# Block sums of the second weights, made where the second and third chunk's tokens lay

## The chip, the cores and the metric

The kernel runs on one core of a Trainium2 chip. Its engines are TensorE (PE in the profile, PEld for its weight loads), VectorE (DVE), ScalarE (ACT), GpSimd (POOL) and SyncE (SP), which here issues all DMA. Each engine takes its instructions strictly in the order in which the program has them. The metric is device time in microseconds (us), lower is better, as a median over runs.

## The reference

The kernel computes a windowed attention and feeds its result to a two-layer feed-forward network:

```python
scores = scale * np.matmul(q, k.transpose(0, 1, 3, 2))      # 8 batches, 8 heads, 576 positions, 64 wide
mask_plain = (rel >= 0) & (rel < window)                    # heads 0 to 3, window 32
mask_dil = (rel >= 0) & (rel < window * dilation) & (rel % dilation == 0)   # heads 4 to 7, dilation 4
scores = np.where(masks[None, :, :, :], scores, -1000000000.0)
attn = softmax(scores); attn_out = np.matmul(attn, v)
...
h = x @ w_in                       # x: 4608 tokens x 512, w_in: 512 x 2048
g = h * np.clip(h + 3.0, 0.0, 6.0) / 6.0
return g @ w_out                   # w_out: 2048 x 512
```

## The kernel before, in words

The 4608 tokens are cut into 12 chunks of 384. Every fp32 operand of the feed-forward part is split into a high and a low part of type fp32r, and a product is three matmuls: high by high, high by low, low by high.

**The first four chunks** are multiplied plainly, in 64 steps of a chunk and one 128-wide slice f of the hidden layer. `gemm1` (L545 to L547) makes `ps_h` in one of two PSUM banks, ScalarE makes `t` by `relu` (L553), VectorE the gate (L556, which reads `ps_h` and so frees its bank), GpSimd the high part `gh`, VectorE the low part `gl` (L564), and two steps later `gemm2` (L595 to L597) uses them. So the gate of a step must be done before the gemm1 two steps later can start.

**The other eight chunks** are multiplied by a Strassen-like scheme of seven products, in groups of two chunks. It needs, besides the weights themselves, sums of blocks of both weight matrices. These are made from the weights on the chip while the first four chunks run, once for each of eight pairs k of slices of both weights (side 0 is `w_in`, side 1 `w_out`): `combo_words` adds high and low part into a tile `v` (L640, two VectorE instructions), `combo_sum` makes four sums in place (L648, four instructions), `combo_high` casts them into a second tile `sh` (L652, ScalarE), `combo_low` leaves the low part in `v` (L657, VectorE), and `combo_out` stores `sh` and `v` into DRAM (L675, two DMAs of 512 KB, into `sums` for side 0 and `rights` for side 1). `combo_plain` stores the plain weights beside them (L666, three DMAs for each pair). Later a ring of eight slots loads all this back (L689, `ring<-sums` and `ring<-rights`), 512 KB at a time.

**Places.** The tokens of the first four chunks lie in three blocks x0, x1, x2 of four tiles each (high and low of two kinds), chunk 3 again in x0. They are allocated once for the whole program (`tokens_tile`, from the pool `const`). When chunk 1 is done, x1's tiles are used for the raw tokens of chunks 4 and 5 (`raw_of`); when chunk 2 is done, x2 takes the operands S2 and S1 of the seven products (`cell`). The block sums take two slots, `v` and `sh`, of the pool `w` (36 slots), which also holds the weights and the ring.

**The order.** A hand-written list orders the first 29 steps. After it every piece of work is an entry of a plan with an engine, a cost, what it comes after, and what slots it takes and gives (`op`, `transfer`). `_in_time` puts the entries of each engine in order by simulating the plan, and the program then issues each engine's instructions in just that order. A plan's costs are guesses of the author's: for instance, a pair's `combo_plain` counts as 1.35 us of SP, and a store as landed 2.6 us after its transfer. On the chip the waits are semaphores: an instruction that writes a place waits until every reader of the place's last content is done, and the instructions behind it on its engine wait with it. DMAs signal eight semaphores in turn, `DMAHW0` to `DMAHW7`.

Of the kernel before, what the change touches and what calls it, by code (L numbers as in the profile page):

```python
# [86 lines left out]
def windowed_attention_ffn(ctx: ExitStack, tc: tile.TileContext, qk, vp, w, mask, out, out_t):  # L87
# [55 lines left out]


    def tokens_tile(block, kind, part, name, dtype=F32R):
        return const.tile([P, 2, CH], dtype, name=name, tag=f"x{block}{kind}{int(part)}")

    xh, xl = ([[tokens_tile(block, kind, part, f"x{block}") for kind in range(2)] for block in range(3)] for part in (1, 0))
    mi = const.tile([P, mask.shape[1]], BF16, name="mi")
# [34 lines left out]
    def w_tile(name, shape, dtype=F32):  # L184
        return wpool.tile([P, *shape], dtype, name=name, tag="w")
# [218 lines left out]
    def raw_of(block, kind):  # L404

        if (block, kind) not in raws:
            if block < 2:
                raws[block, kind] = tokens_tile(1, kind, (xl, xh)[block] is xh, "raw", F32)
            else:
                raws[block, kind] = w_tile("raw", [2, CH])  # L410
        return raws[block, kind]
# [220 lines left out]
    ]  # L632
    KEPT = (T1, T3, T4, T2, R11, R21, R22)

    def combo_words(side, k, i, eng):

        if (side, k) not in combos:
            combos[side, k] = w_tile("v", [4, HALF])
        x, v = (win, wout)[side][2 * k + i], combos[side, k]
        eng.tensor_tensor(  # L640
            out=v[:, 2 * i : 2 * i + 2].rearrange("p a n -> p (a n)"), in0=x[:, 0].bitcast(F32), in1=x[:, 1].bitcast(F32), op=ALU.add
        )
# [5 lines left out]
        eng.tensor_tensor(out=v[:, to], in0=v[:, a], in1=v[:, b], op=op)  # L648

    def combo_high(side, k):  # L650
        hi = w_tile("sh", [4, HALF], F32R)
        nc.scalar.copy(hi, combos[side, k])  # L652
        combos[side, k] = combos[side, k], hi

# [38 lines left out]
    def cell(g, i):  # L693

        if i in (A11, A12, S3):
            x = (i, min(g, 1)) if i == A11 else (i, 0)
            if x not in cells:
                second_place = lambda part, kind: tokens_tile(1, kind, part, "cell")
                small = lambda: w_tile("cell", [2, CH], F32R)
                cells[x] = {  # L700
                    (A11, 0): lambda: [second_place(1, 0), small()], (A12, 0): lambda: [second_place(0, 0), second_place(1, 1)],
                    (A11, 1): lambda: [cells[A11, 0][0], second_place(0, 1)], (S3, 0): lambda: [small(), small()],
                }[x]()
            return cells[x]
        block, kind = {S2: (2, 0), S1: (2, 1), A22: (0, 0), S4: (0, 1)}[i]
        return [x[block][kind] for x in (xh, xl)]

    sources = {}
# [112 lines left out]
    def attend(bs, pools):  # L821
# [38 lines left out]
        for tv in values:  # L860
# [11 lines left out]
            if tv + NLOAD < T:  # L872
                landed_v[tv + NLOAD] = transfer(0.4, 0.77, lambda tv=tv: load_v(tv + NLOAD), [beat])
            pieces = [(n, token // CH) for _, n, _, _, token in spans(tv)]
            x = [*x, ends_of[1]] if any(PLAIN <= c < PLAIN + 2 for n, c in pieces) else x
            touched = {c for n, c in pieces if c >= PLAIN + 2} - {c for c, kind in raw_seen if kind == trios[tv][1]}
            raw_seen.update((c, trios[tv][1]) for c in touched)
            plain = [n for n, c in pieces if c < PLAIN]
# [28 lines left out]
    words, combined, taken = {}, {}, {}  # L907

    def combine(side, k):
        x = op("DVE", 0.69, lambda: combo_words(side, k, 0, nc.vector), takes=[("w", 2, SPARE[side][k])], ahead=LEAD_SUMS)  # L910
        words[side, k] = x = op("DVE", 0.69, lambda: combo_words(side, k, 1, nc.vector), [x], ahead=EVER)
        for i in range(4):
            x = op("DVE", 0.42, lambda i=i: combo_sum(side, k, i, nc.vector), [x], ahead=EVER)
        x = op("ACT", 1.05, lambda: combo_high(side, k), [x], ahead=EVER)
        x = op("DVE", 1.25, lambda: combo_low(side, k, 0, 1, nc.vector), [x], ahead=EVER)
        combined[side, k] = [
            transfer(0.9, 2.0, lambda: combo_out(side, k), [x], gives=[("w", 2)]),
            transfer(1.35, 1.5, lambda: combo_plain(side, k), ahead=EARLY),
        ]

# [58 lines left out]
    def fill(g, free_after):  # L979
# [5 lines left out]
        source = {A11: b11, A12: b21, S2: [t2], S1: [t1], S3: [t3], A22: [t4], S4: b22}  # L985
        after = {A11: [t1], A12: [t4], S2: [t4], S1: [t2], S3: [], A22: [], S4: [t2, t3]}
        order = (S3, A11, S2, S1, A22, S4, A12) if g == 0 else range(PRODUCTS)
        for i in order:
            before_high = [filled.get((0, S3)), *([filled[0, A11], filled[0, S4]] if i == A12 else ()), t1, t2, t3, t4] if g == 0 and i in (A11, A12) else ()
            x = op("ACT", 0.85, lambda i=i: fill_high(g, i), [*source[i], free_after[i], *before_high], takes=[("w", {S3: 2, A11: 1}[i])] if g == 0 and i in (S3, A11) else ())  # L990
            filled[g, i] = op("DVE", 1.1, lambda i=i: fill_low(g, i), [x, *after[i]], gives=() if g == 0 and i in (A11, A12, S3, S4) else SLOT)

    def old_unit(n, tt):
# [288 lines left out]
    with tc.manual_schedule(  # L1282
# [12 lines left out]
            n += kind == "G"  # L1295
        assert len(converted) == 2 * NF

        free = {"work": WORK, "w": SLOTS_W - 2 * NF, "ps_h": 2, "ps_a": 0}
        free["work"] -= 2 * sum(m not in done for m in range(n))
        ends_of, firsts, b = {}, {}, 0  # L1300
        for side in range(2):
# [2 lines left out]
        for m in range(n, len(steps)):  # L1304
# [3 lines left out]
            for late in range(2):  # L1308
                if (m, late) in SPOTS:
                    attend((b, b + 1), (ps_h, ps_a, ps_a, ps_a))  # L1310
                    b += 2
                if not late and m - LAG not in done:
                    second(m - LAG)
        for at in range(RING):
            bring(at)
        spare = {0: ends_of[PLAIN - 1], 1: ends_of[1], 2: ends_of[2]}
# [231 lines left out]
```

## Time and profile before

| what | value |
|---|---|
| runs | 833.76, 834.25, 837.03 us; median 834.25 us |
| the profiled execution | 835.44 us, of it 833.7 us of span |
| TensorE busy | 818.5 us, 98% of the span |
| VectorE, ScalarE, GpSimd busy | 646.6, 579.3, 124.2 us |
| mean granted TensorE clock | 0.996 |
| DMA moved | 214.71 MB, 73.7% of 16 engines' span on the main queue |
| first four chunks | to about 326 us |
| seven products of the first group, first layer | about 326.6 to 398 us |

A row of the page's groups names line, engine, operation, output<-inputs, shapes, count, then busy us and mean ns of one, then the idle time ahead of them and what ended it. A row of a timeline has the start, the us until the last of its instructions ended, engine, line, operation and count; an instruction can start before the end of the one ahead, since engines pipeline. SPq is SyncE's DMA-issuing queue: its durations are the time to issue, not to transfer.

### The profile page before, as it was taken

How to read it: one execution, taken by the hardware profiler on the slowest of the kernel's cores; microseconds unless marked ns; L12 is line 12 of the kernel's file. 1: busy time of each engine (PE TensorE's matmuls, PEld its weight loads, DVE VectorE, ACT ScalarE, POOL GpSimd, SP SyncE). 2: the span in 40 equal slices, each digit the busy share in tenths (PEclk: the TensorE clock that was granted, in tenths of full speed). 3: DMA queues.
4: the chain of work that ended last, by engine and by line, in shares of the span. 5: the costliest groups of instructions: out<-in, count | busy, mean ns of one | idle time of the engine just before them, and what ended most of it. 6: DMA issues, size and time to landing. Idle time of an engine off the chain costs nothing.

```text
span 833.7 us, 22177 instructions
## 1 busy us (share of the span) xinstructions
PE 818.5 (98%) x8732; PEld 772.6 (93%) x8732; DVE 646.6 (78%) x1266; ACT 579.3 (69%) x1406; POOL 124.2 (15%) x184
## 2 busy tenths in 40 slices
PE   7899999999999999999899999999999999999998
PEld 4788999898999998999899999999999999999998
DVE  4899996656777988888899786898676898345983
ACT  4788775344898884988859799855698855345552
POOL 1238442111222221000103002000011000000000
PEclk9899999999999999999999999999999999999999
DMA  8757433262678999999986798787798777897381
GB/s 295 237 205 235 127 113 122 69 228 93 195 249 284 301 344 356 353 395 395 389 282 232 273 346 302 266 315 274 262 316 303 251 266 257 307 359 238 116 297 58
DMA packets 115784, 214.71 MB, mean 258 GB/s; under 512 B 7520, under 2 KB 40288, under 8 KB 115680
## 3 DMA queue, kind: packets, MB, share of 16 engines
q1 hardware_dynamic: 115680, 213.29, 73.7%
q8 instruction: 69, 1.13, 0.6%
q14 instruction: 35, 0.29, 0.1%
HBM read 174.47 MB, written 38.80 MB: 256 GB/s over the span
## 4 chain that ended last, share of the span: by engine, by line
PE 86%; DMA 8%; DVE 3%; ACT 1%; issue 1%; SPq 0%; POOL 0%; DVEq 0%; POOLq 0%
PE ps_o L745 28%; PE ps_x L754 8%; PE ps_x L755 7%; PE ps_x L756 7%; PE ps_h L545 5%; PE ps_o L596 5%; PE ps_o L597 5%; PE ps_o L595 5%; PE ps_h L546 5%; PE ps_h L547 5%; DMA st<-in_w 1%; PE ps_b L246 1%; DMA ring<-sums 1%; DMA ring<-rights 1%; DMA rights<-sh 1%; PE ps_a L246 1%
## 5 line engine op out<-in xcount | busy, mean ns | idle before, releaser
L745 PE MATMUL ps_o<-gh,ring 128*128 128x384 f32 x896 | 230.4, 334 | 1.6 <-DMA ring<-rights 1.2
L745 PEld LDWEIGHTS ps_o<-gh,ring 128*128 128x128 f32 x896 | 161.9, 188 | 2.2 <-DMA ring<-rights 1.5
L745 PE MATMUL ps_o<-gl,ring 128*128 128x384 f32 x448 | 150.0, 335 | 0.9 <-DVE gl L1208 0.9
L1208 DVE TENSOR_TENSOR gl<-g,gh 128x384 fp32r<-128x384 f32 x224 | 116.6, 557 | 18.4 <-ACT gh L1204 15.9
L1204 ACT CAST gh<-g 128x384 fp32r<-128x384 f32 x224 | 105.4, 513 | 34.6 <-PE ps_o L745 26.6
L754 PE MATMUL ps_x<-x,ring 128*128 128x384 f32 x256 | 88.4, 345 | 0.0
L545 PE MATMUL ps_h<-x,wi 128*128 128x384 f32 x256 | 88.2, 345 | 0.0
L546 PE MATMUL ps_h<-x,wi 128*128 128x384 f32 x256 | 86.3, 337 | 0.0
L547 PE MATMUL ps_h<-x,wi 128*128 128x384 f32 x256 | 86.2, 337 | 0.0
L755 PE MATMUL ps_x<-x,ring 128*128 128x384 f32 x256 | 86.1, 336 | 0.0
L756 PE MATMUL ps_x<-x,ring 128*128 128x384 f32 x256 | 86.1, 336 | 0.0
L745 PEld LDWEIGHTS ps_o<-gl,ring 128*128 128x128 f32 x448 | 84.1, 188 | 1.8 <-DVE gl L1208 1.8
L596 PE MATMUL ps_o<-wo,gh 128*128 128x512 f32 x192 | 74.8, 390 | 0.5 <-DVE wo L529 0.5
L595 PE MATMUL ps_o<-wo,gh 128*128 128x512 f32 x192 | 74.9, 390 | 0.0
L597 PE MATMUL ps_o<-wo,gl 128*128 128x512 f32 x192 | 74.7, 389 | 0.0
L553 ACT ACTIVATE t<-ps_h,three 128x384 f32<-128x384 f32 x64 | 37.1, 583 | 50.6 <-PE ps_h L547 50.1
L494 POOL TENSOR_SCALAR va<-st 128x512 f32<-128x512 f32 x32 | 54.7, 1718 | 76.1 <-DMA st<-in_w 63.5
L756 PE MATMUL ps_x<-cell,ring 128*128 128x384 f32 x192 | 64.9, 338 | 0.0
L755 PE MATMUL ps_x<-cell,ring 128*128 128x384 f32 x192 | 64.7, 337 | 0.0
L754 PE MATMUL ps_x<-cell,ring 128*128 128x384 f32 x192 | 64.7, 337 | 0.0
L1173 DVE TENSOR_TENSOR g<-g 128x768 f32<-128x768 f32 x64 | 60.6, 954 | 0.0
L292 ACT ACTIVATE e<-e,mx 128x64 f32<-128x64 f32 x216 | 59.9, 345 | 0.2
(108 smaller groups left out, 1775.4 us busy)
## 6 DMA issues: line engine op xcount, KB each, us to landing
ring<-sums SPq DMA_DIRECT2D x112, 512.0 KB, 8.5
ring<-rights SPq DMA_DIRECT2D x112, 512.0 KB, 6.7
st<-in_w SPq DMA_DIRECT2D x32, 512.0 KB, 4.4
kq<-in_qk SPq DMA_DIRECT2D x39, 416.0 KB, 4.9
v<-in_v SPq DMA_DIRECT2D x39, 390.0 KB, 6.4
sums<-wi SPq DMA_DIRECT2D x24, 256.0 KB, 6.7
rights<-wo SPq DMA_DIRECT2D x24, 256.0 KB, 4.5
out<-o SPq DMA_DIRECT2D x15, 384.0 KB, 2.8
```

Of the source, the lines that this page charges most:

```text
L545: nc.tensor.matmul(ph, lhsT=wt(f, 0)[:, ks], rhs=a, start=(kt == 0), stop=False)
L546: nc.tensor.matmul(ph, lhsT=wt(f, 0)[:, ks], rhs=b, start=False, stop=False)
L547: ins = nc.tensor.matmul(ph, lhsT=wt(f, 1)[:, ks], rhs=a, start=False, stop=(kt == NK - 1))
L595: nc.tensor.matmul(po[c][tt], lhsT=gh[:, rows], rhs=wt(f, 2), start=first, stop=False)
L596: nc.tensor.matmul(po[c][tt], lhsT=gh[:, rows], rhs=wt(f, 3), start=False, stop=False)
L597: return nc.tensor.matmul(po[c][tt], lhsT=gl[:, rows], rhs=wt(f, 2), start=False, stop=(f == NF - 1))
L745: nc.tensor.matmul(banks[part][:, :CH], lhsT=right[:, a, cols], rhs=x, start=(start and not i), stop=(i == 2), skip_group_check=True)
L754: nc.tensor.matmul(bank, lhsT=tile_[:, 0, ks], rhs=h[:, kt], start=(start and kt == 0), stop=False, skip_group_check=True)
L755: nc.tensor.matmul(bank, lhsT=tile_[:, 0, ks], rhs=l[:, kt], start=False, stop=False, skip_group_check=True)
L756: nc.tensor.matmul(bank, lhsT=tile_[:, 1, ks], rhs=h[:, kt], start=False, stop=(kt == 1), skip_group_check=True)
L1204: nc.scalar.copy(two[0], gated_tile(g, q, k))
L1208: nc.vector.tensor_tensor(out=two[1], in0=gated_tile(g, q, k), in1=two[0].bitcast(F32), op=ALU.subtract)
```

## The change

The three blocks of tokens become pools of their own, which are released and allocated anew (`room`, `stage_of`). Block 1 holds chunk 1's tokens, then the block sums of the second weights' pairs 0 to 3, then the raw tokens of chunks 4 and 5. Block 2 holds chunk 2's tokens, then the block sums of the second weights' pairs 4 to 7, then the operands S2 and S1. As a pool of block sums a block has three slots of 4 KB a partition, of which a pair takes two. Side 1 takes no slot of `w` for its sums any more. The raw tokens of chunks 4 and 5 wait for the stores of pairs 0 to 3, and the first group's operands for those of pairs 4 to 7.

```diff
     def tokens_tile(block, kind, part, name, dtype=F32R):
-        return const.tile([P, 2, CH], dtype, name=name, tag=f"x{block}{kind}{int(part)}")
+        return rooms[block].tile([P, 2, CH], dtype, name=name, tag=f"x{block}{kind}{int(part)}")
+
+    def room(block, name, bufs=1):
+
+        if block in rooms:
+            rooms[block].release()
+        side = "right" if block == 2 else "left"
+        rooms[block] = tc.alloc_tile_pool(name=name, bufs=bufs, side=side, reuse_waits="tile")
...
             if block < 2:
+                stage_of(1, 2)
                 raws[block, kind] = tokens_tile(1, kind, (xl, xh)[block] is xh, "raw", F32)
...
+    stage = {1: 0, 2: 0}
+
+    def stage_of(block, n):
+
+        if stage[block] < n:
+            for x in (xh, xl) if n == 1 else ():
+                x[block] = None
+            room(block, f"{'-cr'[n]}{block}", 3 if n == 1 else 1)
+            stage[block] = n
+
+    def combo_tile(side, k, name, dtype=F32):
+
+        if not side:
+            return w_tile(name, [4, HALF], dtype)
+        block = 1 + k // 4
+        stage_of(block, 1)
+        return rooms[block].tile([P, 4, HALF], dtype, name=name, tag="c")
...
-            combos[side, k] = w_tile("v", [4, HALF])
+            combos[side, k] = combo_tile(side, k, "v")
...
-        hi = w_tile("sh", [4, HALF], F32R)
+        hi = combo_tile(side, k, "sh", F32R)
...
-            x = [*x, ends_of[1]] if any(PLAIN <= c < PLAIN + 2 for n, c in pieces) else x
+            if any(PLAIN <= c < PLAIN + 2 for n, c in pieces):
+                x = [*x, ends_of[1], *(combined[1, k][0] for k in range(4))]
...
     def combine(side, k):
-        x = op("DVE", 0.69, lambda: combo_words(side, k, 0, nc.vector), takes=[("w", 2, SPARE[side][k])], ahead=LEAD_SUMS)
+        slots = f"x{1 + k // 4}" if side else "w"
+        x = op(
+            "DVE", 0.69, lambda: combo_words(side, k, 0, nc.vector), takes=[(slots, 1, 1)] if side else [(slots, 2, SPARE[side][k])],
+            ahead=LEAD_SUMS,
+        )
...
-        x = op("ACT", 1.05, lambda: combo_high(side, k), [x], ahead=EVER)
+        x = op("ACT", 1.05, lambda: combo_high(side, k), [x], takes=[(slots, 1)] if side else (), ahead=EVER)
...
-            transfer(0.9, 2.0, lambda: combo_out(side, k), [x], gives=[("w", 2)]),
+            transfer(0.9, 2.0, lambda: combo_out(side, k), [x], gives=[(slots, 2)]),
...
-            x = op("ACT", 0.85, lambda i=i: fill_high(g, i), [*source[i], free_after[i], *before_high], ...
+            x = op("ACT", 0.85, lambda i=i: fill_high(g, i), [*source[i], free_after[i], *(in_room if g == 0 else ()), *before_high], ...
...
-        free = {"work": WORK, "w": SLOTS_W - 2 * NF, "ps_h": 2, "ps_a": 0}
+        free = {"work": WORK, "w": SLOTS_W - 2 * NF, "ps_h": 2, "ps_a": 0, "x1": 0, "x2": 0}
...
+        for c in (1, 2):
+            plan[ends_of[c]].gives.append((f"x{c}", 3))
```

TensorE's order is the same. The others move; in the rows of the change a line number is by 12 to 41 higher for the same code (L683 is `combo_high`'s cast, L652 before; L706 is `combo_out`, L675 before; L697 is `combo_plain`, L666 before; L566 is `relu`, L553 before; L569 is the gate, L556 before).

On SP, around the 24 stores of the plain second weights. Before:

```order
L196 DMA kq<-in_qk 128x832 x2
L205 DMA v<-in_v 128x780 x2
L666 DMA rights<-wo 256x1x256 x24
L689 DMA ring<-sums 128x2x512
L196 DMA kq<-in_qk 128x832
L205 DMA v<-in_v 128x780
L196 DMA kq<-in_qk 128x832
L205 DMA v<-in_v 128x780
L675 DMA sums<-sh 128x4x256
L675 DMA sums<-v 128x4x256
```

and of the change:

```order
L208 DMA kq<-in_qk 128x832 x2
L217 DMA v<-in_v 128x780 x2
L706 DMA rights<-sh 128x4x256
L706 DMA rights<-v 128x4x256
L697 DMA rights<-wo 256x1x256 x24
L720 DMA ring<-sums 128x2x512
L208 DMA kq<-in_qk 128x832
L217 DMA v<-in_v 128x780
L208 DMA kq<-in_qk 128x832
L706 DMA rights<-sh 128x4x256
L706 DMA rights<-v 128x4x256
```

Pair 5's store now stands ahead of the 24, and pair 6's behind them, where a store of side 0 stood. The eight stores of side 1 stood two ahead of this place and six behind it before; now five stand ahead of the 24, one more is the first pair shown here, one is the second, and the last follows three DMAs later.

On ACT, in the steps that follow those stores' time. Before (`relu` is `t<-ps_h`; `e` and `x` belong to the attention):

```order
L553 ACTIVATE t_4627<-ps_h_4576,three_92 128x384 [waits PE_49]
L292 ACTIVATE e_4597<-e_4597,mx_4609 128x64 [waits Activation_49,Pool_49]
L292 ACTIVATE e_4597<-e_4597,mx_4609 128x64
L311 ACTIVATE x_4637<-ps_a_4457,z_4630 128x64 [waits DVE_49,Activation_49]
L311 ACTIVATE x_4637<-ps_a_4457,z_4630 128x64
L292 ACTIVATE e_4597<-e_4597,mx_4609 128x64 x2
L311 ACTIVATE x_4637<-ps_a_4457,z_4630 128x64 x2
L292 ACTIVATE e_4597<-e_4597,mx_4609 128x64 x2
L725 CAST cell_4667<-raw_4593 128x768 [waits DMAHW1_49,DVE_49]
L553 ACTIVATE t_4683<-ps_h_4640,three_92 128x384 [waits PE_49]
```

and of the change (`sh_4734` is pair 7's; `t_4722` and `t_4770` are the `t` of the 59th and 60th `relu` of 64):

```order
L566 ACTIVATE t_4722<-ps_h_4682,three_101 128x384 [waits PE_49,Pool_49]
L304 ACTIVATE e_4648<-e_4648,mx_4702 128x64 [waits Pool_49]
L304 ACTIVATE e_4648<-e_4648,mx_4702 128x64
L323 ACTIVATE x_4728<-ps_a_4508,z_4719 128x64 [waits DVE_49,Activation_49]
L323 ACTIVATE x_4728<-ps_a_4508,z_4719 128x64
L683 CAST sh_4734<-v_4488 128x1024 [waits DMAHW2_49]
L304 ACTIVATE e_4648<-e_4648,mx_4702 128x64 x2
L323 ACTIVATE x_4728<-ps_a_4508,z_4719 128x64 x2
L304 ACTIVATE e_4648<-e_4648,mx_4702 128x64 x2
L566 ACTIVATE t_4770<-ps_h_4737,three_101 128x384 [waits PE_49,Activation_49]
```

Pair 7's cast now stands between two `relu`s, and it waits for a DMA. The tile it writes lies where `sh_4612`, pair 6's, lay. On SP, with buffer numbers, the store of that tile:

```order
L208 DMA kq_4638<-in_qk 128x832 [waits DMAHW7_49,PE_49]
L217 DMA v_4642<-in_v 128x780 [waits DMAHW0_49]
L208 DMA kq_4646<-in_qk 128x832 [waits DMAHW1_49,PE_49]
L706 DMA rights_117<-sh_4612 128x4x256 [waits DMAHW2_49,Activation_49]
L706 DMA rights_117<-v_4170 128x4x256 [waits DMAHW3_49,DVE_49]
L217 DMA v_4670<-in_v 128x780 [waits DMAHW4_49]
L720 DMA ring_4696<-sums_116 128x2x512 [waits DMAHW5_49,Pool_49]
L720 DMA ring_4732<-sums_116 128x2x512 [waits DMAHW6_49]
L706 DMA rights_117<-sh_4734 128x4x256 [waits DMAHW7_49,Activation_49]
L706 DMA rights_117<-v_4488 128x4x256 [waits DMAHW0_49,DVE_49]
```

A DMA takes the semaphore that it waits for in its own turn, so `rights<-sh_4612` is the one that signals `DMAHW2`, and the cast waits for its landing. Pair 6's store (from `sh_4612`, `v_4170`) is the one behind the 24.

More of the change, by code (lines that the diff above doesn't have):

```diff
@@ L145, in tokens_tile @@
     def tokens_tile(block, kind, part, name, dtype=F32R):
-        return const.tile([P, 2, CH], dtype, name=name, tag=f"x{block}{kind}{int(part)}")
+        return rooms[block].tile([P, 2, CH], dtype, name=name, tag=f"x{block}{kind}{int(part)}")
[4 more added lines that the diff above has]
+        rooms[block] = tc.alloc_tile_pool(name=name, bufs=bufs, side=side, reuse_waits="tile")
+    rooms = {}
+    for block in range(3):
+        room(block, f"x{block}")
+        ctx.callback(lambda block=block: rooms[block].release())
     xh, xl = ([[tokens_tile(block, kind, part, f"x{block}") for kind in range(2)] for block in range(3)] for part in (1, 0))
@@ L705, in cell @@
         block, kind = {S2: (2, 0), S1: (2, 1), A22: (0, 0), S4: (0, 1)}[i]
+        if stage[2] < 2:
+            stage_of(2, 2)
+            for part, x in ((1, xh), (0, xl)):
+                x[2] = [tokens_tile(2, kind, part, "x2") for kind in range(2)]
         return [x[block][kind] for x in (xh, xl)]
@@ L987, in fill @@
         order = (S3, A11, S2, S1, A22, S4, A12) if g == 0 else range(PRODUCTS)
+        in_room = [combined[1, k][0] for k in range(4, 8)]
         for i in order:
             before_high = [filled.get((0, S3)), *([filled[0, A11], filled[0, S4]] if i == A12 else ()), t1, t2, t3, t4] if g == 0 and i in (A11, A12) else ()
-            x = op("ACT", 0.85, lambda i=i: fill_high(g, i), [*source[i], free_after[i], *before_high], takes=[("w", {S3: 2, A11: 1}[i])] if g == 0 and i in (S3, A11) else ())
+            x = op("ACT", 0.85, lambda i=i: fill_high(g, i), [*source[i], free_after[i], *(in_room if g == 0 else ()), *before_high], takes=[("w", {S3: 2, A11: 1}[i])] if g == 0 and i in (S3, A11) else ())
             filled[g, i] = op("DVE", 1.1, lambda i=i: fill_low(g, i), [x, *after[i]], gives=() if g == 0 and i in (A11, A12, S3, S4) else SLOT)
```

## The prediction

> **What bounds the kernel now.** I read the page's head and chain of waits first, then TensorE's waits, then the timelines of SP, ACT, DVE and PE around the places where the order changes.
>
> ```profile
> span 833.7 us, 22177 instructions
> PE 818.5 (98%) x8732; PEld 772.6 (93%) x8732; DVE 646.6 (78%) x1266; ACT 579.3 (69%) x1406; POOL 124.2 (15%) x184
> PE 86%; DMA 8%; DVE 3%; ACT 1%; issue 1%; SPq 0%; POOL 0%; DVEq 0%; POOLq 0%
> ```
>
> TensorE is busy for 98% of the span, and its order stays as it was. So the time can change only where TensorE comes to wait, ceases to wait, or gets another clock. Its waits from 330 us to the end (engine, tile, line, releaser: us in total, times, longest):
>
> ```profile
> PE ps_o L745 <- DMA ring<-rights: 1.2, 1, 1.2
> PE ps_o L745 <- DVE gl L1208: 0.9, 3, 0.5
> PE ps_o L745 <- ACT gh L1204: 0.4, 1, 0.4
> ```
>
> They lie in one place, the switch from the first to the second layer of the first group of products. By stretches of time (window, its us, busy us of PE, PEld, DVE, ACT and POOL with counts, TensorE's granted clock, DMA share, GB/s):
>
> ```profile
> 309.00:321.00 12.00, 12.00 (x63) 11.02 (x62) 10.39 (x17) 6.47 (x19) 2.93 (x3) 1.00 1.05 384
> 397.00:400.00 3.00, 1.79 (x11) 1.46 (x10) 2.65 (x8) 2.35 (x6) 0.51 (x1) 1.00 1.05 390
> 400.00:403.00 3.00, 2.46 (x14) 2.14 (x13) 2.45 (x5) 2.59 (x7) 0.51 (x1) 1.00 1.04 396
> 403.00:406.00 3.00, 2.33 (x11) 1.43 (x10) 2.49 (x5) 2.88 (x8) 1.53 (x3) 1.00 1.05 386
> 406.00:409.00 3.00, 3.00 (x18) 3.00 (x19) 2.55 (x5) 2.92 (x7) 1.17 (x4) 1.00 1.05 387
> ```
>
> From 309 to 321 us, where the last plain steps run, TensorE has no gap at all: whatever comes late there is a pure loss. Between 397 and 406 us 11 + 14 + 11 = 36 matmuls run, where at the pace of the next row (18 in 3.00 us) 54 would: 18 short, or 3.0 us. That is all that freer slots and lighter DMA could win at this place. Two places, then: a tight one and a loose one.
>
> **The change part by part.** The same sums are made and the same bytes stored. The arithmetic costs nothing new, and the change is one of places and order.
>
> *The tight place.* Pair 7's cast (the first of its two tiles) is written where pair 6's `sh` lay, for block 2 has three slots and pairs 4 to 7 want eight tiles. Hence it waits until pair 6's store of `sh` has landed. That store now stands on SP behind the 24 plain stores. SP before, at the same places (start, duration, queue, line):
>
> ```profile
> 272.35 0.69 SPq L675 DMA_DIRECT2D sums<-sh  x1
> 273.13 0.74 SPq L675 DMA_DIRECT2D sums<-v  x1
> ...
> 285.29 19.94 SPq L666 DMA_DIRECT2D rights<-wo  x24
> ...
> 307.47 0.56 SPq L205 DMA_DIRECT2D v<-in_v  x1
> 308.13 0.69 SPq L675 DMA_DIRECT2D sums<-sh  x1
> ```
>
> The 24 take 19.94 us of SP's queue, from 285.29 us on, and the first block store behind them goes out at 308.13 us. The plan that set the order counts 1.35 us for each of the eight pairs, 10.8 us in all, so it believes that this store is out some 9 us earlier. With the change two more stores stand ahead of the 24: + (273.91 - 272.35), taken from the pitch of such a pair of issues (the next SP row of the view begins at 273.91), is + 1.56. One `v` load fewer stands between them and pair 6's store: - (308.13 - 307.47) = - 0.66. So it is issued at 308.13 + 1.56 - 0.66 = 309.0 us. How long it takes to land (KB, median us; the first row in the window 306 to 309 us, the second in 167 to 183, the third over the whole span):
>
> ```profile
> sums<-sh SPq DMA_DIRECT2D x1, 512.0 KB, 8.5
> rights<-sh SPq DMA_DIRECT2D x2, 512.0 KB, 3.2
> rights<-sh SPq DMA_DIRECT2D x8, 512.0 KB, 10.2
> ```
>
> I take 8.5, since it is the same transfer at the same place in the same traffic: landed at **317.5 us**. The ends are 3.2 (quiet queue), so 312.2, and 10.2 with up to 2.7 us more if the two stores ahead are themselves slow to land and hold the eight semaphores, so about 322. The Trainium skill ("DMA: Bandwidth & Descriptors", section "Anatomy of one DMA") fits a transfer as 2.0 us and its bytes at 436 GB/s; as an estimate that is 3.2 us for 512 KB. By it the store would land at 312.2 us and the stall worked out below shrinks to 1.6 us; the quiet row agrees with it, the row at this place, 8.5, does not, because of the load on the engines.
>
> Who is queued behind the cast? On ACT it stands between the 59th and the 60th `relu`, ahead of four attention instructions and that `relu`. ACT reaches it at about 305.5 us (row 304.16 below, and the two attention pairs that stand ahead of the cast in the change).
>
> ```profile
> 298.70 1.05 ACT L652 CAST sh<-v 128x1024 fp32r<-128x1024 f32 x1
> ...
> 300.51 0.58 ACT L292 ACTIVATE e<-e,mx 128x64 f32<-128x64 f32 x2
> 300.99 0.51 ACT L311 ACTIVATE x<-ps_a,z 128x64 f32<-128x64 f32 x2
> 301.39 0.59 ACT L292 ACTIVATE e<-e,mx 128x64 f32<-128x64 f32 x2
> ...
> 304.16 0.58 ACT L553 ACTIVATE t<-ps_h,three 128x384 f32<-128x384 f32 x1 [0.57 <-PE ps_h L547]
> ...
> 308.28 0.58 ACT L553 ACTIVATE t<-ps_h,three 128x384 f32<-128x384 f32 x1 [0.40 <-PE ps_h L547]
> ```
>
> So ACT stands still for about 12 us, and the 60th `relu`, at 308.28 before, starts after the landing and the cast (1.05), a pair of `e` (0.48 to the next start), a pair of `x` (0.40) and a pair of `e` (0.48): landing + 2.4 = 319.9 us. The gate is DVE's, and DVE has its own work for pair 7 ahead of it in the order:
>
> ```profile
> 306.48 0.95 DVE L722 TENSOR_TENSOR t<-raw,t 128x768 f32<-128x768 f32 x1
> 308.90 0.55 DVE L556 SCALAR_TENSOR_TENSOR t<-t,ps_h 128x384 f32<-128x384 f32 x1 [1.47 <-ACT t L553]
> ...
> 312.07 1.22 DVE L657 TENSOR_TENSOR v<-v,sh 128x1024 fp32r<-128x1024 f32 x1
> ```
>
> From `relu` to gate it was 308.90 - 308.28 = 0.62, so 317.5 + 2.4 + 0.62 = 320.5. The low part (L657, 1.2 after the cast) and the token difference (L722, 0.95) come to landing + 1.05 + 1.2 + 0.95 = + 3.2 on DVE, 320.7, less some 0.1 for each overlap (the pairs on ACT are 0.58 long and 0.48 apart): nearly the same. I take 320.55. The gate takes 0.55 and ends at 321.1 us. It frees the PSUM bank for the 62nd gemm1, which began at 314.25:
>
> ```profile
> 306.00 0.34 PE L545 MATMUL ps_h<-x,wi 128*128 128x384 f32 x1
> ...
> 314.25 0.34 PE L545 MATMUL ps_h<-x,wi 128*128 128x384 f32 x1
> ...
> 326.63 0.34 PE L754 MATMUL ps_x<-cell,ring 128*128 128x384 f32 x1
> ```
>
> **The stall of TensorE is 321.1 - 314.25 = 6.9 us**, with 1.6 and about 11 for the two ends of the landing. Nothing later takes it back: from 326.63 us the seven products follow, whose rows run without a wait up to 397 us. What is late next is not late alone: the 61st `relu` and gate follow at once while TensorE does the 62nd gemm1, since their own gemm1 has been done since 312 us.
>
> *The clock after the stall.* The trace of before has one such pause, at the start, where TensorE worked for little more than half of six us:
>
> ```profile
> 24.00:26.00 2.00, 1.13 (x32) 0.83 (x32) 1.90 (x5) 1.03 (x4) 0.27 (x1) 1.00 0.86 249
> 26.00:28.00 2.00, 1.16 (x24) 0.73 (x22) 1.93 (x7) 1.18 (x4) 0.00 (x0) 1.00 0.94 374
> 28.00:30.00 2.00, 1.00 (x20) 0.62 (x28) 1.63 (x3) 1.86 (x4) 1.53 (x1) 0.88 0.19 66
> 30.00:32.00 2.00, 2.00 (x97) 1.72 (x84) 1.23 (x3) 1.44 (x5) 0.00 (x0) 0.50 0.70 190
> ...
> 36.00:38.00 2.00, 2.00 (x14) 1.97 (x13) 2.00 (x6) 1.74 (x4) 0.00 (x0) 0.91 0.39 55
> ```
>
> After it the clock stands at 0.50 until the window 36 to 38 us: 0.48 us of half clock in 28 to 30 ((1 - 0.88) / 0.5 x 2), 6 us, and 0.36 us in 36 to 38, together 6.8 us, which lose 3.4 us of work. The stall of 6.9 us is about as long as that pause, but part of the half clock falls into the stall itself, where it costs nothing. Bounds 0 and 3.4; I take the middle, **+ 1.7**. The Trainium skill ("TensorE: Matmul & The Clock Gate", section "What's actually happening") has the clock halved after an idle window of about 3.4 us and whole again after about 3.4 us of sustained work; as an estimate that loses 1.7 us here, and the 6.8 us of the row are twice its figure.
>
> *The loose place.* Six block stores of side 1 go out between 341 and 392 us (the windows 341 to 366.5 and 366.5 to 392):
>
> ```profile
> rights<-sh SPq DMA_DIRECT2D x4, 512.0 KB, 10.2
> rights<-sh SPq DMA_DIRECT2D x2, 512.0 KB, 11.0
> ```
>
> In the change's order three of side 0 stand there instead, and no pair of side 1 takes slots of `w` from the ring. The ring's first `rights` loads can come earlier, so the wait of 1.2 us on them and those on `gl` and `gh` that follow may go. Bounds 0 and 3.0 us; I take **- 2.0**, as the DMA share there is 1.05 in each row and will not fall at once.
>
> *The other edits at nothing.* The pools' releases add waits of the raw tokens of chunks 4 and 5 for the stores of pairs 0 to 3, and of the first operands S2 and S1 for those of pairs 4 to 7. The former stores stand ahead of the 24; the latter end with pair 7's, which goes out after the cast, some 1 us behind it, and the cells that it covers are not the first that the products take. If that cover fails, it costs 1 to 3 us at 326 us (rival below).
>
> **Sum.** + 6.9 + 1.7 - 2.0 = + 6.6 us. Against its own time the profiled execution goes from 835.44 us (833.7 of span and 1.7 around it) to 842.0. It lies 1.19 above the median of 834.25, which gives 840.9; I say 841.0.
>
> **The rivals.**
>
> *The store lands fast.* If the block stores ahead of the 24 empty the queue, pair 6's store has the quiet 3.2 us. The stall is 1.6 us, too short for the clock, and the loose place gives 2 to 3: 834.25 + 1.6 - 2.5 = 833.4. For it: the two stores moved ahead of the 24 are gone from the traffic of 309 us. Against: DMA is at 1.05 of its share in the row 309 to 321. From a landing below about 4 us on, the change is a draw. Chance 0.10.
>
> *It does what it says.* The cast isn't held: the slot that it takes is free, or ACT reaches it only when the store has landed. Then freer slots bring the ring's loads early and only the loose place counts: 834.25 - 2 to - 3 = 831.3 to 832.3, faster or not slower. It decides from the point where the landing comes ahead of about 310.6 us (317.5 less the 6.9). For it: the later gain exists, 3.0 us of missing matmuls. Against: the wait of the cast on `DMAHW2` in the order, and 19.94 us of SP between. Chance 0.07.
>
> *A second wait.* The first operands in block 2 wait for pair 7's store, which stands behind two ring loads; at 10.2 us from issue it lands about 1 to 3 us after the products want it. Sum + 6.6 + 1 to 3: 842 to 844, or up to 846.5 with the late end of the landing. Chance 0.08.
>
> The forecast itself has 0.75.
>
> **How the numbers follow.** The forecast's own range goes from a landing of 6 us (stall 4.4, clock 0.5, gain 3: 836) to one of 10.2 with the window held (stall 8.6 to 11, clock 1.7 to 3.4, gain 2: 846.5). The two fast rivals, 0.17, lie mostly below, which with a little above leaves 0.2 out: 836 to 846.5. A change of 0.5%, 4.2 us, is what a measurement of this kernel tells from none. Slower than 838.4: nearly all of the forecast and the second wait, 0.78. Within: the fast landing and the forecast's low edge, 0.17. Faster than 830.1: the change doing what it says with more than the loose place holds, 0.05.
>
> **What would show it.** TensorE's waits should have a new one of about 7 us at 314 us on the 62nd gemm1, released by DVE's gate or through ACT; ACT should stand about 12 us ahead of a cast `sh<-v`, released by the store of `rights<-sh`, and that store's row on SP should start near 309 us with 8 to 9 us to landing. The granted clock should fall for some us after 321 us, and the windows 397 to 406, shifted by the delay, should hold more than 36 matmuls. No stall at 314 us would overthrow the sum; one of 1 to 2 us says the landing was mis-sized; a clock of 1.00 throughout takes the 1.7 away; the same 36 matmuls later take the gain away.

## The result: slower by 1.2%, through one stall

The changed kernel takes 844.65 us (843.60 to 847.29, 4 runs), against 834.50 us before (833.76 to 837.03, 4 runs). The ratio is 1.0121, with a 95% interval from 1.0089 to 1.0152. The profiled execution took 844.56 us, 842.8 of it span. The page's head and its chain:

```profile
span 842.8 us, 22173 instructions
PE 822.9 (98%) x8732; PEld 777.1 (92%) x8732; DVE 643.6 (76%) x1266; ACT 577.1 (68%) x1406; POOL 124.5 (15%) x184
PE 94%; DMA 2%; DVE 2%; ACT 1%; SPq 0%; issue 0%; DVEq 0%
```

DMA has fallen from 8% to 2% of the chain of waits, so the transfers hold the end less than before; all the same the kernel is slower. From 140 us to the end the view of TensorE's waits has one line left (tile, line, releaser: us in total, times, longest):

```profile
PE ps_h L558 <- DVE t L569: 7.3, 1, 7.3
```

The waits on `ring<-rights`, `gl` and `gh` are gone, and one wait on a gate has come. Follow it back through the four timelines of the changed kernel (start, us, engine, line, operation, in brackets the idle time ahead and what ended it). SP:

```profile
288.12 21.46 SPq L697 DMA_DIRECT2D rights<-wo  x24
...
312.11 0.60 SPq L706 DMA_DIRECT2D rights<-sh  x1
```

ACT:

```profile
306.25 0.58 ACT L566 ACTIVATE t<-ps_h,three 128x384 f32<-128x384 f32 x1 [2.12 <-PE ps_h L560]
...
320.12 1.04 ACT L683 CAST sh<-v 128x1024 fp32r<-128x1024 f32 x1 [12.40 <-DMA rights<-sh]
...
322.43 0.56 ACT L566 ACTIVATE t<-ps_h,three 128x384 f32<-128x384 f32 x1
```

DVE and PE:

```profile
321.19 1.23 DVE L688 TENSOR_TENSOR v<-v,sh 128x1024 fp32r<-128x1024 f32 x1 [11.96 <-ACT sh L683]
...
323.20 0.55 DVE L569 SCALAR_TENSOR_TENSOR t<-t,ps_h 128x384 f32<-128x384 f32 x1
```

```profile
323.81 0.69 PE L558 MATMUL ps_h<-x,wi 128*128 128x384 f32 x1 [7.29 <-DVE t L569]
```

The store stands behind the 24, the cast stands 12.40 us for its landing, the 60th `relu` stands behind the cast, the gate behind that `relu`, and TensorE's 62nd gemm1 behind the gate. Then the clock, by stretches of time (window, us, busy us of PE, PEld, DVE, ACT, POOL, granted clock, DMA share, GB/s):

```profile
315.00:321.00 6.00, 1.52 (x7) 0.94 (x5) 0.00 (x0) 0.88 (x1) 0.00 (x0) 0.96 1.04 349
321.00:324.00 3.00, 0.19 (x1) 0.19 (x2) 2.81 (x4) 2.87 (x11) 0.11 (x1) 0.50 1.05 394
324.00:326.00 2.00, 2.00 (x7) 2.00 (x8) 1.60 (x4) 0.00 (x0) 0.99 (x1) 0.50 1.08 381
326.00:328.00 2.00, 2.00 (x9) 1.96 (x8) 1.97 (x6) 1.59 (x5) 0.81 (x2) 0.68 1.07 352
328.00:330.00 2.00, 2.00 (x11) 1.68 (x11) 2.00 (x4) 1.42 (x7) 0.87 (x1) 1.00 1.06 397
```

TensorE works again from 323.81 us, and its clock is half for 0.19 + 2 + 1.28 us of that time ((1 - 0.68) / 0.5 x 2 = 1.28), 3.5 us in all. That loses 1.7 us of work. The clock was half from about 320.5 us on already ((1 - 0.96) / 0.5 x 6 = 0.5 us in the first row), inside the stall, where it costs nothing. At the start of the second layer, which before had only 36 matmuls in its three windows:

```profile
405.00:411.00 6.00, 6.00 (x36) 6.00 (x35) 5.46 (x11) 5.82 (x15) 0.97 (x3) 1.00 0.93 315
411.00:414.00 3.00, 3.00 (x19) 3.00 (x18) 2.94 (x6) 2.91 (x8) 1.95 (x3) 1.00 1.03 364
```

there is no gap. So far the time has three parts: a stall, its echo in the clock, and a gain. How large each is can be read by comparing the starts of the same matmuls. TensorE's order is the same in all kernels here, 8732 matmuls, so the delay of the n-th one against the first profile of before can be taken apart by stage. This table gives, for each kernel, how much the delay grew (us) in each stretch; its rows below the first belong to the experiments.

| kernel | start to 1400th (77 us) | to 3940th (313 us) | to 4050th (330 us) | to 5100th (394 us) | to 5200th (416 us) | to the last (830 us) |
|---|---|---|---|---|---|---|
| the change | +0.76 | +1.35 | +9.21 | +0.06 | -3.85 | +0.66 |
| E1, price 2.7 (15 stores) | -1.04 | +1.32 | +1.56 | +0.15 | -3.85 | +0.78 |
| E2, pair 7 in w | -0.32 | +1.41 | +10.36 | +0.16 | -3.86 | +0.79 |
| E3, block 1 alone | -0.20 | +1.74 | +0.09 | +0.06 | -3.85 | +0.66 |
| E4, block 2 alone | +1.90 | +1.27 | +7.27 | +0.04 | +4.15 | +0.65 |
| E5, before again | -0.99 | -0.21 | 0.00 | 0.00 | -0.73 | 0.00 |
| E6, price 2.1 (21 stores) | -0.50 | +1.04 | +6.67 | +0.06 | -3.85 | +0.69 |
| E7, price 2.4 (18 stores) | +1.31 | +1.74 | +5.71 | +0.05 | -3.85 | +0.66 |
| E8, late plain stores (12) | -1.38 | +1.17 | +0.10 | +0.06 | -3.85 | +0.65 |
| E9, the pools alone | +1.52 | +0.89 | +0.10 | +0.15 | -0.71 | +0.79 |
| E10, E8 with more stores | -0.23 | +1.57 | +0.10 | +9.63 | -3.65 | +0.68 |
| E11, E8 in other places | +1.43 | +1.12 | +0.06 | -0.14 | -3.86 | -0.40 |

The first column is scatter from run to run: the kernel before itself differs by 1.0 there. In the other columns the kernels agree within some tenths where their orders agree.

### The profile page after: what moved, and what is told of

It reads as the page before. It is cut to its first block, busy times and chain, and to the rows that moved or that the text cites. A ratio compares the mean times of both kernels' runs of the same rounds, so it can differ in the third digit from the quotient of the medians.

```text
span 842.8 us, 22173 instructions
## 1 busy us (share of the span) xinstructions
PE 822.9 (98%) x8732; PEld 777.1 (92%) x8732; DVE 643.6 (76%) x1266; ACT 577.1 (68%) x1406; POOL 124.5 (15%) x184
## 4 chain that ended last, share of the span: by engine, by line
PE 94%; DMA 2%; DVE 2%; ACT 1%; SPq 0%; issue 0%; DVEq 0%
PE ps_o L780 28%; PE ps_x L789 10%; PE ps_x L790 9%; PE ps_x L791 9%; PE ps_h L558 5%; PE ps_o L609 5%; PE ps_o L608 5%; PE ps_h L559 5%; PE ps_h L560 5%; PE ps_o L610 5%; PE ps_b L258 2%; PE ps_b L240 1%; PE ps_a L258 1%; PE ps_a L240 1%; DMA ring<-sums 1%; PE ps_a L250 1%
## 5 line engine op out<-in xcount | busy, mean ns | idle before, releaser
L558 PE MATMUL ps_h<-x,wi 128*128 128x384 f32 x256 | 89.7, 350 | 7.5 <-DVE t L569 7.5
L559 PE MATMUL ps_h<-x,wi 128*128 128x384 f32 x256 | 87.0, 340 | 0.0
L560 PE MATMUL ps_h<-x,wi 128*128 128x384 f32 x256 | 87.0, 340 | 0.0
L566 ACT ACTIVATE t<-ps_h,three 128x384 f32<-128x384 f32 x64 | 36.9, 580 | 46.2 <-PE ps_h L560 46.1
```

Of the source, the lines that this page charges most:

```text
L558: nc.tensor.matmul(ph, lhsT=wt(f, 0)[:, ks], rhs=a, start=(kt == 0), stop=False)
L559: nc.tensor.matmul(ph, lhsT=wt(f, 0)[:, ks], rhs=b, start=False, stop=False)
L560: ins = nc.tensor.matmul(ph, lhsT=wt(f, 1)[:, ks], rhs=a, start=False, stop=(kt == NK - 1))
```

## The experiments

**E1, the true price of the plain stores.**

```diff
-            transfer(1.35, 1.5, lambda: combo_plain(side, k), ahead=EARLY),
+            transfer((1.35, 2.7)[side], 1.5, lambda: combo_plain(side, k), ahead=EARLY),
```

> One number of the change's plan differs: a pair's three plain stores of the second weights count as 2.7 us of SP (what the 24 took in the trace of the change: 21.46 / 8) in place of 1.35. In the order that follows, pair 6's store stands behind 15 of the 24 plain stores instead of all, so it goes out some 8 us earlier (nine stores at 0.89), near 304 us, and lands near 312. Theory (the stall of 7.29 us at TensorE's 62nd gemm1 comes from that landing alone): no wait at the 62nd gemm1, full clock there, and the shorter waits at the start of the second layer stay away as in the change: 844.65 - 9.3 = 835.4 us, or down to 831 if the 2.0 us that the change's profile lost before 305 us was no effect of the change. Rival A (the lost waits of the second layer were a gift of the stall, in which the DMA queue ran on for 9 us while TensorE stood): the stall goes, but the 3.85 us come back: 839. Rival B (the loss is the pools' releases or the early waits, not this landing): it stays at 842 to 845.

Measured: 837.25 us (835.02 to 838.93), ratio to before 1.0025 (1.0006 to 1.0044), so 7 us less than the change. Its one wait of TensorE is new. SP and ACT of E1:

```profile
302.26 0.38 SPq L706 DMA_DIRECT2D rights<-sh  x1
...
317.27 0.96 SPq L706 DMA_DIRECT2D rights<-v  x1
```

```profile
309.62 1.05 ACT L683 CAST sh<-v 128x1024 fp32r<-128x1024 f32 x1 [2.86 <-DMA rights<-sh]
...
324.48 1.57 ACT L760 CAST x<-t 128x768 fp32r<-128x768 f32 x2 [3.39 <-DMA rights<-v]
```

```profile
PE ps_x L790 <- DVE cell L764: 0.8, 1, 0.8
```

The cast still waits, but only for 2.86 us, which ACT has to spare. The stall at the 62nd gemm1 is gone, and the gain of 3.85 us stays, which speaks against rival A. Rival B falls too. But one place further on the same thing happens on a small scale: the casts of the first operands into block 2 wait for pair 7's store, whose second DMA left at 317.27, behind the last of the plain stores. This costs 1.56 us (the table's third column), of which the view of waits names 0.8. The measured median is 1.8 us above the expected 835.4, while the profiled execution took 835.02; where that difference lies is open.

**E2, pair 7 in w.**

```diff
-        if not side:
+        if not side or k == 7:
             return w_tile(name, [4, HALF], dtype)
```

(with the plan's slots for pair 7 changed in the same way)

> The change, but pair 7's two tiles are taken from the pool w as before, so that its cast waits for no store of pair 6. The order of SP stays as in the change up to pair 6's store, behind all 24 plain stores. Theory: the stall at the 62nd gemm1 goes without the store being earlier, for it was the slot that coupled them: 835 us, with most of the later gain (3.85 us) left, 831 at the least. Rival A (gift of the stall): 838 to 839. Rival B (the stall is SP's or the DMA queue's own lateness, whatever slot the cast has): 842 to 845, with the wait at the 62nd gemm1 still there.

Measured: 844.26 us (839.84 to 846.31), ratio 1.0105 (1.0065 to 1.0145). My theory said 835, and it was wrong in this form. TensorE's wait and ACT of E2:

```profile
PE ps_h L558 <- DVE t L569: 8.0, 1, 8.0
```

```profile
321.58 0.83 ACT L760 CAST x<-t 128x768 fp32r<-128x768 f32 x1 [13.34 <-DMA rights<-sh]
```

Pair 7's cast is no longer there, but the planner, which still believes that pair 6's store is out early, now puts the cast of an operand of the seven products into block 2 at the same place of ACT's order, between the 59th and the 60th `relu`. It waits for the very same store. So the cause is not pair 7: it is a store that is issued late, and any user of its place that the plan puts ahead of a `relu`.

**E3 and E4, one block alone.** E3 sends pairs 4 to 7 to `w` as before, E4 pairs 0 to 3 (`if not side or k >= 4`, `if not side or k < 4`, each with the plan's slots and waits to match).

> Block 1 alone: pairs 0 to 3 in the second chunk's tokens' place, pairs 4 to 7 in w as before. Theory (only block 2 brings the stall, since only there a pair's second tile reuses a place whose store stands behind the 24): no wait at the 62nd gemm1; half of the slots are given to the ring, so between before and before less half of the gain: 832.5 to 834.5 us. Rival (the early waits of block 1 for the stores cost the 2.0 us that the profile of the change lost before 305 us): 836 to 837.

> Block 2 alone: pairs 4 to 7 in the third chunk's tokens' place, pairs 0 to 3 in w as before. Pair 6's store stands at once behind the 24 plain stores, one store of side 0 among them, and pair 7's cast stands between the 59th and the 60th relu and waits for it. Theory: the stall is there, at the 62nd gemm1, by 5 to 7.5 us, and the clock after it costs 1 to 2: 840 to 844 us. Rival (the two blocks must come together for the stall): 833 to 835.

Measured: E3 834.27 us (832.68 to 836.40), ratio 0.9996 (0.9981 to 1.0012); E4 850.79 us (850.05 to 851.30), ratio 1.0190 (1.0163 to 1.0217). E4's two longest waits of TensorE between 300 and 420 us, and its cast:

```profile
PE ps_o L780 <- ACT gh L1245: 4.2, 2, 2.7
PE ps_h L558 <- DVE t L569: 3.7, 1, 3.7
```

```profile
317.45 1.04 ACT L683 CAST sh<-v 128x1024 fp32r<-128x1024 f32 x1 [9.14 <-DMA rights<-sh]
```

Block 2 alone brings the stall (3.7 us there, 5 to 7.5 expected) and block 1 alone doesn't. And block 1 alone brings the whole gain at the second layer, -3.85, where I had expected half; block 2 alone turns it into a loss of 4.15. In E4 the last block stores come late: five pairs of stores still leave after 341 us, against three in the change and none in E3 (six before). E4 is thus a third way to be slow, which neither theory had: 4.15 us lost at the second layer, which with 7.27 makes it slower than the change. Against the change that is 8.0 us at this place: the waits of 4.2 us on `gh`, and behind them a clock that is half from 413.2 to 420.0 us. Why `gh` was late there is open.

**E5, before again.**

> The kernel before, profiled again. All four variants so far, and the change, were up to 1.3 us later than the first profile of before on the way from the 1800th to the 3800th matmul (156 to 297 us) without a wait of TensorE that the view of waits names (the change 0.62 us, the others 0.51, 0.70, 1.22 and 0.63). If that is the chip or the run and no effect of the edits, this profile is 0.4 to 0.7 us later there too than the first one; if it is the edits, it is within 0.1 us of the first one. In both cases the 36 matmuls with 3.85 us of waits at 397 to 406 us should be there again, and no wait at 314 us.

Measured: 833.52 us. From the 1400th to the 3940th matmul it is 0.21 us ahead of the first profile, so the 0.9 to 1.7 us that all variants lose there look like the edits', not the run's (this is one execution). The waits of the second layer are there again, and cost 0.73 us less than in the first profile:

```profile
PE ps_o L745 <- DMA ring<-rights: 0.5, 1, 0.5
PE ps_o L745 <- DVE gl L1208: 0.4, 2, 0.3
PE ps_o L745 <- ACT gh L1204: 0.4, 1, 0.4
```

So the gain of the change at that place is 3.1 to 3.85 us, depending on the execution of before that it is held against.

**E6 and E7, the dose.** As E1, with prices of 2.1 and 2.4: pair 6's store behind 21 and 18 of the plain stores.

> The plain stores' price in the plan is 2.1 us in place of 1.35: pair 6's store stands behind 21 of the 24 plain stores; ACT's and DVE's order around it stay nearly the same. Theory (the stall is the store's place on SP, 0.89 us for each plain store ahead of it): the store goes out 2.5 to 2.7 us earlier than in the change, the stall of the 62nd gemm1 is 7.3 - 2.7 = 4.6 us (4 to 5.5), and the half clock after it costs 1 to 2 us. Rival (the planner's other effects took the stall away, not the place of the store): no stall, or the whole 7.3.

> The same with a price of 2.4 us: pair 6's store behind 18 of the 24. Theory: stall 7.3 - 5.4 = 1.9 us (0.5 to 2.5), and no loss of clock behind so short a stall; then some 1 to 2 us at 326 us, where the first operands wait for pair 7's store, as with 15 of 24 (1.5). Rival as with 21.

Measured, one execution each: 839.64 and 841.97 us. E6's waits of TensorE, then its SP and ACT:

```profile
PE ps_x L789 <- ACT cell L760: 2.5, 1, 2.5
PE ps_h L558 <- DVE t L569: 1.0, 1, 1.0
PE ps_x L790 <- DVE cell L764: 0.9, 1, 0.9
```

```profile
307.64 0.81 SPq L706 DMA_DIRECT2D rights<-sh  x1
...
319.42 0.49 SPq L706 DMA_DIRECT2D rights<-v  x1
```

```profile
313.13 1.05 ACT L683 CAST sh<-v 128x1024 fp32r<-128x1024 f32 x1 [5.23 <-DMA rights<-sh]
...
328.42 1.56 ACT L760 CAST x<-t 128x768 fp32r<-128x768 f32 x2 [5.34 <-DMA rights<-v]
...
330.37 0.82 ACT L760 CAST cell<-raw 128x768 fp32r<-128x768 f32 x1
```

With 21 stores ahead the stall at the 62nd gemm1 is 1.0 us, not the 4.6 I had expected, and with 18 it is nothing, not 1.9. The cast tells why. Taken from the delay that TensorE has at that point, the store left 2.9 us earlier than in the change, as expected (312.11 - 2.1 against 307.64 - 0.5), but it also landed faster (313.13 - 307.64 = 5.5 us from issue, 8.0 in the change), and from landing to the gemm1 it was 0.9 us less (315.96 - 313.13 = 2.8 us, 3.7 in the change), since DVE has no token difference of 0.95 us between pair 7's low part and the gate here: 7.3 - 2.9 - 2.5 - 0.9 = 1.0. So the stall does go with the store's place, but the time to land is no constant. And a second surprise: the loss falls far less than the stall. From the change over E6 and E7 to E1 the table's third column goes 9.21, 6.67, 5.71, 1.56. (That E7's total lies above E6's comes from the first two columns and from 0.9 us behind the last matmul.) The first operands' wait for pair 7's store, 1.56 us in E1, is 2.5 + 0.9 us in E6, since the first products' own `cell<-raw` stands behind the held casts on ACT, and then the clock is half again. E7 has the same, one of its waits and the windows after them:

```profile
PE ps_x L789 <- ACT cell L760: 2.6, 1, 2.6
```

```profile
334.00:336.00 2.00, 2.00 (x9) 1.77 (x10) 2.00 (x4) 2.00 (x4) 0.00 (x0) 0.79 1.11 405
336.00:338.00 2.00, 2.00 (x6) 1.55 (x5) 1.71 (x3) 1.14 (x3) 1.00 (x1) 0.50 0.24 91
338.00:340.00 2.00, 2.00 (x100) 1.31 (x99) 1.89 (x4) 0.10 (x1) 0.07 (x1) 0.86 0.00 0
```

0.84 + 2 + 0.56 = 3.4 us of half clock after waits of 2.6 and 0.9 us. The price of the two together is 5.71 us in E7's row of the table, 3.5 of waiting and some 2 of clock and what it delays.

**E8, the plain stores of pairs 4 to 7 made late.** E1's price, and in addition:

```diff
+            for k in range(4, 8):
+                plan[combined[1, k][1] - 1].after.append(combined[1, 7][0] - 1)
             for _, i, _ in _in_time(plan, free):
```

> The change with the price of 2.7 us, and the plain stores of pairs 4 to 7 made to follow pair 7's block store: pair 6's store stands behind 12 of the 24, and pair 7's five DMAs later with no plain store between. With a price of 2.7 alone the stall was gone, but the first operands waited for pair 7's store (landed at 324.5 us), which cost 1.5 us at 326 us. Theory: neither stall nor that wait, the 3.85 us of the second layer's start still gained: 835.0 - 3.85 + 0.5 to 1.5 (lost before 305 us) = 831.5 to 833. Rival (the ring's first loads, now among the late plain stores, come late): waits for ring<-sums of 1 to 5 us after 326 us, 833 to 838.

Measured: 834.24 us (831.44 to 835.89, 12 runs), ratio 0.9993 (0.9980 to 1.0006). The view names no wait of TensorE from 140 us on. Pair 6's store leaves at 300.20, pair 7's at 309.36, and the two columns where the other versions lost show +0.10 and -3.85. The rival's waits for `ring<-sums` do not come. Still the time is only that of before: 1.2 us above what I expected at most, where two columns take back 1.17 and 0.65. Against E5 in place of the first profile, the columns behind the first add up to a gain of 0.9 us, and the medians differ by 0.4 (834.24 against 834.66 in the same series), which the interval does not tell from none.

**E9, the pools alone.** All block sums in `w` as before (`if not side or True`), the three pools kept, the waits for the stores taken out of the plan.

> Only the three pools for the tokens are kept of the change: the block sums of both sides take slots of w as before, and no wait is added. Between the 1400th and the 3800th matmul (77 to 297 us) every kernel with the change's pools was later by 1.0 to 1.8 us against the first profile of before, and the second profile of before was not (-0.2); the first two of nine matmuls of many gemm2 steps take 6 or 7 ns longer there (228 to 235 ns). Theory (the places of the tiles in memory that the pools bring, not the sums): this kernel is later by 1.0 or more there as well, with those same matmuls slow, and by some 0.5 us from 415 us to the end; its waits at 397 to 406 us are those of before. Rival (the sums' traffic or waits in the new places): within 0.2 us of before there.

Measured, one execution: 838.18 us. The pools alone cost 0.89 us from the 1400th to the 3940th matmul and 0.79 us from the 5200th to the last; its second layer waits as that of before does (-0.71, as E5). No wait is named in those stretches. It is the matmuls themselves that follow each other a little slower: of 153 successions from a gemm2 matmul of L596 (before's line) to the next matmul, between the 1400th and the 3800th, the sum is 34.68 us in both profiles of before, 34.93 in E9 and 34.94 in the change; of 336 from L755 to L756 in the products after 415 us, 58.58 and 58.55, against 59.12 and 59.03. Not all are slower: some take 231 to 234 ns where they took 226 or 227, the others are as before.

**E10, more traffic.** E8, and with it, behind six of the ring's loads of the first layer:

```diff
+            if at in (11, 13, 15, 17, 19, 21):
+                transfer(0.9, 2.0, lambda: more_stores(at), [ring_landed[at] - 1], ahead=EVER)
```

where `more_stores` issues two stores of 512 KB from the mask's tile.

> The version with the late plain stores, with twelve more stores of 512 KB each to a place that nobody reads, behind six of the ring's loads of the first layer (issued between some 341 and 392 us), as many as side 1's block stores that stood there before. They take no slot of w. Theory (the 3.85 us at 397 to 406 us were lost to the traffic of late block stores, which makes the first loads ring<-rights issue later and land in 10 us in place of 6.5): waits of 2 to 4 us for ring<-rights, gl and gh come back at the start of the second layer. Rival (they were lost to slots of w that the block sums held): the start of the second layer stays without a wait, under 0.5 us.

Measured, one execution: 843.97 us. TensorE's waits:

```profile
PE ps_b L258 <- DMA v<-in_v: 5.2, 1, 5.2
PE ps_x L795 <- DMA ring<-sums: 2.2, 1, 2.2
```

The stores cost 9.63 us, but not where I had expected it: TensorE waits until 379 and 399 us for a load of the attention and one of `ring<-sums`, 7.4 us in all, with the clock half from 376.7 to 383.5 us, and by the time it comes to the second layer nothing waits there (-3.65). So this traffic is enough to cost more than the whole gain without taking a slot of `w`; that it was the traffic and not the slots that made before's waits at 397 us is not shown by it. What speaks for it is the landing time of the ring's loads in the profiles. `ring<-rights` from 392 to 420 us, before, in E4 (slow there) and in the change:

```profile
ring<-rights SPq DMA_DIRECT2D x14, 512.0 KB, 10.2
```

```profile
ring<-rights SPq DMA_DIRECT2D x11, 512.0 KB, 9.9
```

```profile
ring<-rights SPq DMA_DIRECT2D x14, 512.0 KB, 6.6
```

E10's own loads took 10.0 us there without a wait, but TensorE came 9.6 us later to them. What speaks against the number of slots is E3 against E4: each keeps four pairs' sums out of `w`, and one has the whole gain, the other a loss. They differ, among other things, in how many block stores leave after 341 us. That is an argument, and no run here changes the slots alone.

**E11, other places for the pools.** E8 with the pools of `w`, `work`, the loads and the small tiles allocated with `side="right"`, in the reverse order, so that the token blocks lie at the low end as before.

> The version with the late plain stores, with the pools of w, work, the loads and the small tiles allocated from the upper end of the memory, so that the three token blocks lie low (6.8 to 44 KB a partition, where they lay at 1.2 to 38 KB before; in the change at 192 to 229 KB) and w begins at 44.1 KB (43.7 before, 6.8 in the change). All orders stay. Theory (the 0.8 us lost from 77 to 297 us and the 0.6 to 0.8 us from 415 us on, which the pools alone brought, come from these places): both are back to within 0.2 us of the kernel before, no wait of TensorE from 140 us on, and the time is 1.5 us below that of the late version (834.24): 832.7, below before's 834.7. Rival (another trait of the pools, as their own waits): as slow in both stretches as the change, 834.2.

Measured: 832.63 us (829.43 to 835.47, 12 runs) against 835.12 for before in the same series, ratio 0.9965 with an interval from 0.9947 to 0.9983. This is the version that beats both kernels: 0.35% below before, and 12 us below the change as measured in its own series. Of the two stretches one is back: from the 5200th matmul to the end it is 0.40 us ahead of before's first profile (L755 to L756: 58.43). The other is not: +1.12 to the 3940th, and L596 to the next 35.09. So the places of the tiles matter, but which property of them does isn't settled.

## Why the prediction was right, and what in it was not

I forecast 841.0 us (836.0 to 846.5) and slower with a chance of 0.78; measured were 844.65. By the prediction's own steps:

- **The wait of pair 7's cast** on pair 6's store behind the 24: as predicted, on the engine and between the `relu`s that were named. ACT stood 12.40 us where "about 12" was written. E3, which has no such cast, has no stall.
- **The landing**, put at 317.5: it came at 320.1. The store went out at 312.1 in place of 309.0, since the 24 began 1.3 us later than the sum has it (288.12 against 285.29 + 1.56) and took 21.46 us instead of 19.94; issue to landing took 8.0 us (8.5 taken). TensorE was 2.1 us later as well, so little of it counts. The 8.5 was a lucky pick in part: pair 6's store took 4.4 us to land in E4 and 9.5 in E2.
- **From landing to the gemm1**: 321.1 - 317.5 = 3.6 predicted, 323.81 - 320.12 = 3.7 measured.
- **The stall** of 6.9 us: 7.29 measured.
- **The clock**, 1.7 us taken between 0 and 3.4: 1.7 by the windows, and 9.21 - 7.29 = 1.9 with the first slow matmuls by the table. That part of the half clock would fall into the stall was right: it lasted 6.8 us (320.5 to 327.3), as at the kernel's start, and 3.3 of them cost nothing. The Trainium skill ("TensorE: Matmul & The Clock Gate", section "What's actually happening") has the whole clock back after about 3.4 us of sustained work; the 3.5 us of half clock after the stall agree with it. In other traces it came later or sooner, 2.9 us (E6), 4.7 us (E7) and 5.7 us (E4, second layer) after the last wait. E7's half clock came after waits of 2.6 and 0.9 us, each below the idle window of about 3.4 us that the Trainium skill states there.
- **The gain**, -2.0 with 3.0 as its bound: mis-sized. It is 3.85 us against the first profile and 3.1 against the second. The bound was read wrongly from right rows: a window counts every matmul that overlaps it, and matmuls last 0.34 us at 0.17 us apart, so about two in each window's count had begun in the window before. Of the 36 some 30 began there, and 9.00 us at 0.172 would have held 52: 22 x 0.172 = 3.8 us.
- **Not in the sum at all**: the places of the tokens. The pools alone cost 0.89 us before 313 us and 0.79 after 415 (E9). The prediction priced the pools' releases as waits and their allocation as nothing. Nor is the kernel's end in the sum: from the last matmul's start to the end of the span the change took 4.5 us and before 3.6, for a reason that is open.
- **The second wait**, given 0.08 as a rival: not in the change, since TensorE is so late that pair 7's store has landed (issued at 321.19, landed 6.3 us later, and the products begin near 338). But it was the next in the row. In E1, E6 and E7, where the stall is shorter or gone, it costs 1.6 us (E1) to 3.5 us (E7) of waiting. The prediction's reason for putting it at nothing, that the cells it covers are not the first that the products take, was no protection: in E6 the first matmul of the products waits for the cast at 330.37, which stands on ACT behind the covered ones.

Sum in the profile: 0.76 + 1.35 + 9.21 + 0.06 - 3.85 + 0.66 = 8.19 at the last matmul, and with the 0.9 behind it 9.1 in the span. The forecast of + 6.6 was too low by the tokens' places (1.35 + 0.66, of which the pools alone bring 1.7), by 0.76 of scatter in the first stage, 0.9 at the end and 0.6 in stall and clock, and too high by the gain (1.85). The places and the gain nearly cancel, which was luck, so the total came out better than its parts.

The rivals "lands fast" and "does what it says" are out: 8.0 us to land, and a stall that E8 takes away with the change's memory saving kept.

## What to carry to other kernels

When an order is planned from prices, look up in the trace what the plan's cheap items really take: here eight groups of stores at 1.35 us each took 2.5 to 2.7, and the error of 9 to 11 us came out at the first instruction that reused a place behind them: 12.4 us of standing on ACT, 7.3 on TensorE. An in-order engine turns a wait for one place into a wait of everything behind it, so a reuse that looks free belongs only after the last urgent instruction, or its store ahead of the bulk. Removing the one waiting instruction (E2) is not a repair; moving the store is (E8), and the second-latest store is then the next to look at.

## What the runs showed of the hardware that was not expected

- Where tiles lie changes the pace of matmuls by a few per cent of single instructions: about 227 to 233 ns for some gemm2 matmuls with no wait named, 0.9 us over the first part and 0.8 over the last with the pools alone (E9). Other places brought the last part back and not the first (E11). The cause is open.
- A wait of 2.6 us and one of 0.9 us shortly after it were followed by 3.4 us of half clock (E7), while one of 0.8 us alone was not (E1: the windows from 324 to 332 us all have 1.00).
- Half clock comes in whole pieces: up to the last matmul every stretch of it in the traces here lasted 3.4, 6.8 or 10.2 us (E7 335.2 to 338.6 us, the change 320.5 to 327.3, E2 317.6 to 327.8).
- A store of 512 KB took 5.5 us (E6) or 8.0 us (the change) to land at nearly the same place of the order, issued 2.9 us apart by TensorE's progress.
